# QK^T in 64-row matmuls from wave 40 on, and a TensorE order that plans for changes of row count

One core of one Trainium2 chip; the metric is the device time of one execution in microseconds (us), the median of the runs of one kernel. "Before" is an already tuned attention kernel, "after" the same kernel with the change.

## The reference

```python
B, H, S, D = 1, 32, 2048, 640          # Dh = D // H = 20
def reference(q, k, v, t):             # q, k, v: (1, 32, 2048, 20) bf16; t: (32,)
    eps = 1e-6
    qn = q / (jnp.sqrt((q * q).sum(axis=-1, keepdims=True)) + eps)
    kn = k / (jnp.sqrt((k * k).sum(axis=-1, keepdims=True)) + eps)
    logits = jnp.einsum('bhqd,bhkd->bhqk', qn, kn) * t[None, :, None, None]
    attn = _softmax(logits, axis=-1)
    return jnp.einsum('bhqk,bhkd->bhqd', attn, v)
```

There are 32 heads of 2048 x 2048 logits, each from a contraction over only 20 channels (padded to 32). The exp of 134 million logits is most of the work.

## The kernel before

Logits are made in units of 128 keys x 512 queries. Two engines turn them into weights. ScalarE takes "waves" of three units (a 128x1536 exp from the PSUM tile `psA`, which has two slots). VectorE takes three or four "tiles" of four units per head through one PSUM bank, `psD`, and computes exp with integer arithmetic. TensorE makes the logits (QK) and multiplies the weights with v (PV, four 128*32 matmuls side by side into `psO`; in the trace of before all four start within 10 ns in the median). Every instruction is a task in a small list scheduler, run when the program is built. It gives each engine a static, in-order list, so an engine that falls behind its plan makes the others wait (in the trace of before VectorE waits 18.6 us for `psD`).

A unit's 32 channels lie in one of four 32-partition bands g. The moving operand `qz[g]` holds q in band g and zeros in the other bands, so a unit can be computed with 32, 64 or 128 array rows with the same result. In a wave of three units two lie in different halves of the array: this "pair" runs as two 64-row matmuls side by side (their starts are 3 ns apart in the median of that trace). The third, the "single", uses 128 rows, as do VectorE's units.

```python
    # the scheduler picks the next task of an engine by priority (lower first)
                _, _, t = heapq.heappop(ready[e])
                t.start = now
                t.end = now + t.dur
                if e == "PE":
                    kind = t.name[:2]                 # "qk" or "pv"
                    if kind != last_pe[0]:
                        t.end += 0.09                 # planned cost of a change
                    last_pe[0] = kind
    # ... cut ...
        def qk_mm(eng, h, r, g, dst, rows):
            # ... cut: choice of slot, lhsT (keys) ...
            p0 = 32 * g // rows * rows
            ps = slice(p0, p0 + rows)
            mov = qz[bt][ps, g, :] if rows > 32 else qkT[bt][ps, 0:512]
            # ... cut ...
            return eng.matmul(dst, lhsT, mov, tile_position=(p0, 0))
    # ... cut: add_wave(w), with pair = two neighbouring units in different halves ...
            qks = [add("PE", f"qkA{w}", lambda e, tk, part=part: f_qk(e, part, 32 if plain else 64 if part is pair else 128),
                       PE_MM * (1 if plain or part is pair else len(part)), deps, due_a(us[0]) - 100) for part in parts]
    # ... cut: add_dgroup, VectorE's tile j, unit g ...
                    qk = add("PE", f"qkD{j}.{g}", lambda e, tk, h=h, r=r, g=g, j=j: qk_mm(
                        e, h, r, g, psD[:, :], 128 if j else 32), PE_MM, dep, due - 50)
    # ... cut: loads of q (in four parts), k and v, all issued in order from one queue ...
                    lds[h].append(dma("SP", f"ldq{h}", dst, src, war, pri, f"q{b}", lat=2.5))
```

## Time and profile before

| | before |
|---|---|
| time, median of 3 runs (lowest to highest) | 755.69 us (755.17 to 755.82) |
| span of the profiled run, mean granted TensorE clock | 753.2 us, 1.000 |
| exp waves; shortest and median distance of their starts | 539; 1330 and 1330 ns |
| loss of ScalarE: sum of (distance - 1330 ns), before wave 40 / from wave 40 on | 3.7 / 14.3 us |
| distances over 1400 ns | 100 |

In this trace ScalarE never starts two waves closer than 1330 ns, so I take the sum of what the distances have above it as what ScalarE lost to waiting. The starts are those of the trace's timeline.

Five lines of the kernel before's timeline (start us, us, engine, line, op, rows*columns of the array used, shapes, count; in brackets the idle time before and what ended it) show what a change of shape costs.

```profile
402.12 0.10 PEld L415 LDWEIGHTS psA<-qz,qkT 64*128 64x128 bf16 x2 [0.26 <-ACT p_ring L489]
402.13 0.39 PE L415 MATMUL psA<-qz,qkT 64*128 64x512 bf16 x2
...
402.45 0.39 PE L415 MATMUL psA<-qz,kR 128*128 128x512 bf16 x1
...
402.77 0.40 PE L424 MATMUL psO<-p_ring,vaug 128*32 128x512 bf16 x4
...
402.99 0.39 PE L424 MATMUL psO<-ss,vaug 128*32 128x512 f16 x4
```

From the pair to the single, and from the single to PV, the starts are 0.32 us apart; from PV to PV they are 0.22 us apart. (The record of one matmul is 0.39 us long and those of PV start 0.22 us apart, so records overlap; I count the distances of the starts.) The waits view puts this time down to "issue", for which it sees no releaser (us in total, times, longest).

```profile
PEld psA L415 <- issue: 169.9, 711, 0.4
PEld psA L415 <- ACT p_ring L489: 124.4, 356, 1.0
...
DVE xt L522 <- PE psD L415: 18.6, 41, 1.2
```

### The profile page before, as it was taken

Reading aid. Unit: us, or ns where it says so; the run is one execution under the profiler, and the core shown is the slowest. Engines: PE = TensorE matmul, PEld = TensorE weight load, DVE = VectorE, ACT = ScalarE, POOL = GpSimd, SP = SyncE. Lnnn points to the kernel's source line nnn. Section 1 sums busy time; section 2 is a strip of 40 time slices with the busy share of each in tenths; the row PEclk is TensorE's granted clock in tenths of the full one; section 3 lists DMA queues with packets and bytes.
Section 4 is the critical chain, followed back from the end, with each engine's and each line's share of the span. In section 5 each row is a group of like instructions: output and inputs, shape, how many; then the busy total and the mean of one; then the engine's idle time right before and its main releaser. Section 6 shows DMA issues by size and latency. Waiting matters only on the chain.

```text
span 753.2 us, 12434 instructions
## 1 busy us (share of the span) xinstructions
PE 702.4 (93%) x4960; PEld 194.6 (26%) x4960; DVE 719.6 (96%) x1209; ACT 731.7 (97%) x541; POOL 9.2 (1%) x24
## 2 busy tenths in 40 slices
PE   1999999999999999999999999999999999999997
PEld 0222222222222222222222222222222222222222
DVE  7799999999999999999999999999999999999997
ACT  3899999999999999999999999999999999999997
POOL 4000000000000000000000000000000000000000
PEclk9999999999999999999999999999999999999999
DMA  5533242323423242250323413234141332413000
GB/s 76 84 38 54 42 75 33 73 22 68 53 37 72 24 81 29 55 66 19 78 24 66 55 29 71 21 66 54 37 76 9 82 39 46 70 28 72 5 5 5
DMA packets 197929, 36.49 MB, mean 48 GB/s; under 512 B 173680, under 2 KB 197872, under 8 KB 197872
## 3 DMA queue, kind: packets, MB, share of 16 engines
q1 hardware_dynamic: 197728, 35.62, 29.6%
q8 instruction: 39, 0.64, 0.4%
q14 instruction: 18, 0.15, 0.1%
q10 hardware_dynamic: 144, 0.08, 0.1%
HBM read 7.87 MB, written 2.62 MB: 14 GB/s over the span
## 4 chain that ended last, share of the span: by engine, by line
ACT 59%; PE 23%; DVE 15%; DMA 1%; issue 1%; SPq 0%; DVEq 0%
ACT p_ring L489 59%; PE psA L415 11%; PE psO L424 8%; DVE xt L522 6%; PE psD L415 5%; DVE tt L536 4%; DVE mm L534 1%; DVE ee L530 1%; DVE ss L532 1%; DVE sq L320 1%; DVE rs_sum L322 1%; DMA kR<-kx 1%; SPq L234 0%; DVE qkn L348 0%; DMA qk_sb<-in_k_dram 0%
## 5 line engine op out<-in xcount | busy, mean ns | idle before, releaser
L489 ACT ACTIVATE p_ring<-psA 128x1536 bf16<-128x1536 f32 x539 | 730.2, 1523 | 15.7 <-PE psA L415 14.5
L415 PE MATMUL psA<-qz,kR 64*128 64x512 bf16 (+1 forms) x1209 | 319.0, 389 | 13.9 <-ACT p_ring L489 10.7
L522 DVE TENSOR_SCALAR xt<-psD 128x512 int16<-128x512 f32 x432 | 295.4, 684 | 23.1 <-PE psD L415 18.6
L424 PE MATMUL psO<-p_ring,vaug 128*32 128x512 bf16 x1616 | 152.1, 388 | 0.6 <-DVE oT L436 0.4
L415 PEld LDWEIGHTS psA<-qz,kR 64*128 64x128 bf16 (+1 forms) x1209 | 83.4, 94 | 225.3 <-issue 128.4
L415 PE MATMUL psA<-qz,qkT 64*128 64x512 bf16 (+1 forms) x392 | 128.6, 388 | 4.0 <-ACT p_ring L489 3.2
L536 DVE TENSOR_TENSOR tt<-xt,mm 128x2048 f16<-128x2048 f16 x108 | 131.0, 1213 | 0.2
L415 PE MATMUL psD<-qz,kR 128*128 128x512 bf16 x321 | 124.0, 386 | 6.0 <-DVE xt L522 3.8
L530 DVE TENSOR_SCALAR ee<-xt 128x2048 int16<-128x2048 int16 x108 | 73.7, 682 | 0.4
L534 DVE TENSOR_SCALAR mm<-xt 128x2048 int16<-128x2048 int16 x108 | 73.8, 684 | 0.0
L532 DVE TENSOR_SCALAR ss<-xt 128x2048 int16<-128x2048 int16 x108 | 73.7, 683 | 0.0
L424 PEld LDWEIGHTS psO<-p_ring,vaug 128*32 128x32 bf16 x1616 | 38.5, 94 | 84.6 <-issue 74.9
L415 PEld LDWEIGHTS psA<-qz,qkT 64*128 64x128 bf16 (+1 forms) x392 | 31.3, 94 | 68.9 <-issue 41.5
L415 PEld LDWEIGHTS psD<-qz,kR 128*128 128x128 bf16 x321 | 31.0, 97 | 65.8 <-DVE xt L522 43.6
L424 PE MATMUL psO<-tt,vaug 128*32 128x512 f16 x432 | 42.8, 386 | 3.4 <-DVE tt L536 2.0
L424 PE MATMUL psO<-ee,vaug 128*32 128x512 f16 x432 | 43.1, 389 | 1.5 <-DVE ee L530 1.3
L415 PE MATMUL psD<-qz,qkT 128*128 128x512 bf16 x107 | 41.5, 388 | 2.2 <-DVE xt L522 1.1
L424 PE MATMUL psO<-ss,vaug 128*32 128x512 f16 x432 | 42.7, 386 | 0.1
L320 DVE TENSOR_TENSOR sq<-qk_sb 128x640 f32<-128x640 bf16 x32 | 26.0, 813 | 0.9 <-DMA qk_sb<-in_q_dram 0.9
L322 DVE TENSOR_REDUCE rs_sum<-sq 128x32 f32<-128x640 f32 x32 | 25.7, 804 | 0.1
L348 DVE TENSOR_TENSOR qkn<-qk_sb,rs_r 128x640 bf16<-128x640 bf16 x31 | 25.2, 815 | 0.1
L436 DVE STREAM_TRANSPOSE oT<-psO 128x512 f32<-128x512 f32 x32 | 22.7, 709 | 2.1 <-PE psO L424 2.1
(36 smaller groups left out, 117.9 us busy)
## 6 DMA issues: line engine op xcount, KB each, us to landing
kR<-qkT SPq DMA_DIRECT2D x62, 96.0 KB, 2.1
qz<-qkT SPq DMA_DIRECT2D x128, 32.0 KB, 1.9
kR<-qkT SPq DMA_DIRECT2D x62, 64.0 KB, 2.0
qk_sb<-in_k_dram SPq DMA_DIRECT2D x32, 80.0 KB, 2.1
vaug<-in_v_dram SPq DMA_DIRECT2D x32, 80.0 KB, 3.3
qk_sb<-in_q_dram SPq DMA_DIRECT2D x124, 20.0 KB, 2.5
out_dram<-o_stage SPq DMA_DIRECT2D x31, 80.0 KB, 1.9
kR<-qkT SPq DMA_DIRECT2D x62, 32.0 KB, 1.9
```

What stands on the lines that cost most here:

```text
L320: s1 = dv("sq", lambda e, tk, x=x: e.tensor_tensor(sq[:, :, :], x[:, :, :], x[:, :, :], ALU.mult), 0.86, lds[h] + last_sum)
L322: sums.append(dv("sum", lambda e, tk, i=i: e.tensor_reduce(rs["sum"][:, 2 * R * i:2 * R * (i + 1)], sq[:, :, :], AXIS_X, ALU.add), 0.86, [ ...
L348: norm[h] = dv("norm", lambda e, tk, x=x, b=b, i=i: e.tensor_tensor(qkn[b][:, :, 0:D], x[:, :, :], bc(rs["r"][:, 2 * R * i:2 * R * (i + 1) ...
L415: return eng.matmul(dst, lhsT, mov, tile_position=(p0, 0))
L424: last = eng.matmul(psO[32 * g:32 * g + 32, :], vaug[h % NV][:, r_of(g), :], rhs_of(g), start=start, stop=False, skip_group_check=True, ti ...
L436: trO[h] = add("DVE", f"tr{h}", lambda e, tk: e.transpose(oT[:, :, :].rearrange("p r d -> p (r d)"), psO[:, :]), 0.63, [lambda: pv_users[h ...
L489: act[w] = add("ACT", f"exp{w}", lambda e, tk: e.activation(p_ring[:, p0 * 512:p0 * 512 + n], psA[:, slot * WAVE * 512:slot * WAVE * 512 + ...
L522: t1_prev[0] = add("DVE", f"t1.{j}.{g}", lambda e, tk, o=o: e.tensor_scalar(xt[sx][:, o:o + 512], psD[:, :], X_MUL, X_ADD, ALU.mult, ALU.a ...
L530: te = dv("e", lambda e, tk: e.tensor_scalar(ee[se][:, 0:w], x, 0x7C00, KE_BITS, ALU.bitwise_and, ALU.bitwise_or), 0.533, t1s + old("e", NE))
L532: t5 = dv("s", lambda e, tk: e.tensor_scalar(ss[se][:, 0:w], x, float(SHIFT - 4096), None, ALU.add), 0.533, t1s + old("s", NE))
L534: tm = dv("m", lambda e, tk: e.tensor_scalar(mm[sm][:, 0:w], x, 0x3FF, 0x3800, ALU.bitwise_and, ALU.bitwise_or), 0.533, t1s + old("m", NM))
L536: tT = dv("T", lambda e, tk: e.tensor_tensor(tt[se][:, 0:w], x.bitcast(FP16), mm[sm][:, 0:w].bitcast(FP16), ALU.mult), 1.067, [tm] + old(" ...
```

## The change

Intent: from wave 40 on all QK of ScalarE's waves, and from tile 8 on all QK of VectorE, is done with 64 rows, so that TensorE doesn't change its row count between pair and single. The scheduler learns that 64-row QK ("q2"), 128-row QK ("qk") and PV ("pv") are three kinds, and it prefers a task of the kind that ran last if its priority is no more than 0.3 heads later. VectorE's QK loses its very high priority.

```diff
+    SWITCH = 0.3
 # ... cut ...
-                _, _, t = heapq.heappop(ready[e])
+                if e == "PE":
+                    x = min(ready[e], key=lambda r: (r[0] + (0.0 if r[2].name[:2] == last_pe[0] else self.SWITCH), r[1]))
+                    ready[e].remove(x)
+                    heapq.heapify(ready[e])
+                    t = x[2]
+                else:
+                    _, _, t = heapq.heappop(ready[e])
 # ... cut ...
+    LIGHT = 40
+    LD = 8
 # ... cut ...
+            light = w >= LIGHT
-            qks = [add("PE", f"qkA{w}", lambda e, tk, part=part: f_qk(e, part, 32 if plain else 64 if part is pair else 128),
+            qks = [add("PE", f"q{'2' if part is pair or light else 'k'}A{w}", lambda e, tk, part=part: f_qk(e, part, 32 if plain else 64 if part is pair or light else 128),
 # ... cut ...
-                    qk = add("PE", f"qkD{j}.{g}", lambda e, tk, h=h, r=r, g=g, j=j: qk_mm(
-                        e, h, r, g, psD[:, :], 128 if j else 32), PE_MM, dep, due - 50)
+                    qk = add("PE", f"q{'k' if j < LD else '2'}D{j}.{g}", lambda e, tk, h=h, r=r, g=g, j=j: qk_mm(
+                        e, h, r, g, psD[:, :], (128 if j < LD else 64) if j else 32), PE_MM, dep, due - 0.5)
```

More of the change, by code (lines that the diff above doesn't have):

```diff
@@ L44 @@
     SEM_LAT = {"PE": 0.18, "ACT": 0.15, "DVE": 0.10, "POOL": 0.15, "SP": 0.0}
+    SWITCH = 0.3
     def __init__(self):
         self.tasks = []
+        self.nsw = 0
     def add(self, eng, name, fn, dur, deps=(), pri=0.0, lat=0.0, dma=None):
@@ L100, in schedule @@
                         t.end += 0.09
+                        self.nsw += 1
                     last_pe[0] = kind
```

## The prediction

The 96 ns are the difference of two distances in the trace of before, 322 - 226 ns. 45 + 24 = near 69 us of TensorE time, and 9.7 us, about two thirds of the 14.3 us of late waves, taken off 755.7 us gives 746.0 us.

> **What bounds the kernel now.** Three engines are almost full: ScalarE 97%, VectorE 96%, TensorE 93% (busy shares of the page). ScalarE sets the floor. In the timeline its 539 exp waves start no closer than 1330 ns, and more than half of the intervals are exactly that. 538 x 1.330 = 715.5 us, and the measured distance from the first to the last start is 733.5 us, so only 18.0 us is lost. Of that, 3.7 us falls before wave 40, where the change starts, and 14.3 us after it. What lies before the first wave (14.1 us) and after the last (4.2 us) stays. So at most about 14 us (1.9%) can be won. VectorE has similar room: in the stretch from 30 to 747 us it is busy 694 of 717 us, and its largest wait is for TensorE's psD (18.6 us, 41 times, by the waits).
>
> **What the losses come from.** TensorE runs late. Starts of successive matmuls in the timeline are 226 ns apart when the row/column shape stays (128*32 after 128*32, or 128*128 after 128*128), and about 322 ns when it changes: 64-row pair to 128-row single 322 (501 times), PV to 64-row pair 322 to 332, single to PV 308 to 320. [...] About 1670 changes of this kind cost some 160 us of TensorE. The plan knows of 0.09 us at a change between QK and PV, but of none between 64 and 128 rows, so the real TensorE falls behind its static order, and ScalarE and VectorE wait.
>
> **What the change does.** From wave 40 on (93% of the waves) QK has one shape. The change inside a wave goes (465 x 96 ns = 45 us) and that from a 128-row single to the next pair (about 250 x 96 ns = 24 us): near 69 us of TensorE time. A wave's QK becomes available 96 ns sooner. A lone 64-row matmul should take as long as a 128-row one. Planning with a switch penalty should also save some QK/PV changes. VectorE's QK loses its near-absolute priority over PV (due-50 becomes due-0.5), which may delay a few psD.
>
> **On the critical path.** Per wave TensorE needed about 1234 of 1330 ns; it will need about 1100 (estimates from slot counts times 226 ns plus changes times 96 ns). Nearly all of the 69 us is therefore off the critical path; what counts is how many of the 14 us of late waves go. I expect about two thirds: in-order queues and the single psD buffer keep some waits, and VectorE must then be 98% full.
>
> **Prediction.** 746.0 us (-1.3%), 80% range 741.5 to 752.5. Faster by over 2%: 0.06; within 2%: 0.91; slower by over 2%: 0.03.
>
> **What would show it.** TensorE busy falls from 93% towards 85 to 88%; single-after-pair spacing 322 becomes 226 ns; intervals of exp over 1400 ns fall from 100 to a third or half; VectorE's wait for psD falls under 10 us; exp still 1330 ns; DMA unchanged; ScalarE's share reaches 98%.
>
> **What would make it wrong.** If 64-row matmuls on the same half can't hide their weight load (spacing stays near 320 ns), nothing is won. If the new order delays psD or PV so that VectorE starves, it is flat or slower.

## More of the kernel before

From the page of the kernel before: span, busy time of each engine with its share and its instructions, the granted clock in 40 slices (9 is 90% or more), the chain that ended last, and two groups (busy us, mean ns of one, then idle time before them and what ended it).

```profile
span 753.2 us, 12434 instructions
...
PE 702.4 (93%) x4960; PEld 194.6 (26%) x4960; DVE 719.6 (96%) x1209; ACT 731.7 (97%) x541; POOL 9.2 (1%) x24
...
PEclk9999999999999999999999999999999999999999
...
ACT 59%; PE 23%; DVE 15%; DMA 1%; issue 1%; SPq 0%; DVEq 0%
...
L489 ACT ACTIVATE p_ring<-psA 128x1536 bf16<-128x1536 f32 x539 | 730.2, 1523 | 15.7 <-PE psA L415 14.5
L415 PE MATMUL psA<-qz,kR 64*128 64x512 bf16 (+1 forms) x1209 | 319.0, 389 | 13.9 <-ACT p_ring L489 10.7
```

Three engines are nearly full at once, and TensorE holds 23% of the chain: waves are often released by it and not by ScalarE itself.

## The result, and the profile after

| | before | after |
|---|---|---|
| time, median (lowest to highest) | 755.43 us (754.94 to 755.82, 4 runs) | 757.07 us (755.01 to 766.85, 4 runs) |
| ratio of the fast runs | 1 | 1.0013, 95% interval 0.9992 to 1.0034 |
| mean granted clock | 1.000 (profiled run) | 0.979, 0.979, 0.973 (fast); 0.955 (the run of 766.85 us, slow) |
| loss of ScalarE, before wave 40 / from wave 40 on | 3.7 / 14.3 us | 2.9 / 14.7 us |
| distances over 1400 ns | 100 | 40 |

A ratio is the mean time of one kernel's fast runs over that of the other's of the same rounds, so it is not quite the ratio of the medians quoted. The slow run is left out of what follows.

So nothing was won: 0.1% slower, within noise. Yet the mechanism is there. First the same lines of the page, of the kernel after.

```profile
span 753.0 us, 12422 instructions
...
PE 646.4 (86%) x4954; PEld 160.9 (21%) x4960; DVE 718.0 (95%) x1209; ACT 727.3 (97%) x541; POOL 9.2 (1%) x24
...
PEclk9999999999999899999989999988999999999999
...
ACT 85%; PE 5%; DVE 4%; SPq 2%; DMA 2%; issue 1%; ACTq 0%; DVEq 0%
...
L502 ACT ACTIVATE p_ring<-psA 128x1536 bf16<-128x1536 f32 x539 | 725.7, 1776 | 20.2 <-PE psA L427 18.5
L427 PE MATMUL psA<-qz,kR 64*128 64x512 bf16 (+1 forms) x1208 | 290.0, 392 | 51.5 <-ACT p_ring L502 44.1
```

TensorE is 56 us less busy, and now waits for ScalarE. Its part of the chain fell from 23% to 5%. But the row of the clock has eights in it that were not there before. Two lines of the timeline of the kernel after show pair and single.

```profile
239.54 0.39 PE L427 MATMUL psA<-qz,kR 64*128 64x512 bf16 x2
...
239.76 0.38 PE L427 MATMUL psA<-qz,qkT 64*128 64x512 bf16 x1
```

They are now 0.22 us apart, although the single uses rows that the pair has just used. The waits view of the kernel after:

```profile
PEld psA L427 <- ACT p_ring L502: 215.1, 469, 1.2
...
PEld psA L427 <- issue: 19.2, 57, 0.8
...
DVE xt L535 <- PE psD L427: 15.4, 37, 0.9
...
DVE sq L332 <- DMA qk_sb<-in_q_dram: 4.4, 3, 2.2
```

The unexplained "issue" time fell from 169.9 us to 19.2 us: so most of these waits stood at the changes of row count that are gone. The fall is more than what was saved. A wait of 0.23 us at a change also holds what the weight loader idles without one (some 0.13 us, an estimate: 226 ns between starts less 94 ns of loading), and a part is now put down to ScalarE (215.1 us, 124.4 before). The last line is new in size (0.9 us in 3 waits before): twice VectorE waits about 2 us for a late load of q.

Where did the gain go? The windows view of the kernel after, in stretches of 3.4 us around 384 us, gives busy us (and instructions) of PE, PEld, DVE, ACT and POOL, then the granted clock, DMA share and GB/s.

```profile
380.50:383.90 3.40, 2.99 (x23) 0.76 (x23) 3.30 (x6) 3.40 (x4) 0.00 (x0) 1.00 0.78 82
383.90:387.30 3.40, 1.29 (x9) 0.27 (x8) 1.16 (x3) 3.40 (x3) 0.00 (x0) 1.00 0.67 42
387.30:390.70 3.40, 3.02 (x16) 0.49 (x16) 3.07 (x6) 1.86 (x3) 0.00 (x0) 0.50 0.00 0
390.70:394.10 3.40, 2.06 (x18) 0.54 (x15) 3.40 (x5) 3.40 (x3) 0.00 (x0) 0.99 0.00 0
394.10:397.60 3.50, 3.50 (x22) 0.71 (x21) 3.29 (x9) 2.90 (x3) 0.00 (x0) 0.51 0.02 5
```

In the stretch from 383.9 us VectorE waits 2.24 us for q, its QK, in order in TensorE's list, is held up behind it (2.89 us before the weight load of `psD` at 387.68 us, by the timeline), and TensorE is busy for only 1.29 of 3.40 us. In the next stretch the granted clock is 0.50, and ScalarE is busy for 1.86 of 3.40 us. After one more lean stretch (390.7 us: 2.06 us busy) the clock falls again. A waiting load isn't needed for this, as the same view around 90 us shows.

```profile
86.90:90.30 3.40, 2.68 (x23) 0.72 (x20) 3.23 (x5) 3.40 (x4) 0.00 (x0) 1.00 0.54 109
90.30:93.70 3.40, 1.95 (x17) 0.43 (x11) 3.40 (x6) 3.40 (x4) 0.00 (x0) 1.00 0.27 68
93.70:97.20 3.50, 3.50 (x23) 0.61 (x20) 3.50 (x7) 3.50 (x3) 0.00 (x0) 0.51 0.33 82
```

Here VectorE and ScalarE are busy all through the second stretch; TensorE had less to do (1.95 us busy), and it lost its clock for the next 3.4 us.

The trace's clock record has 30.7 us at half clock in six stretches (3.4, 3.4, 6.8, 3.4, 3.4 and 10.2 us), not counting the start and the end of the program. The record of before has none. Only 1.0 and 0.5 occur in the two records. In that of after every stretch between the first fall and the one at the end of the program, at half or at full clock, is a multiple of 3.413 us (half clock 3.413, 6.827 and 10.240 us; full clock from 3.413 to 238.933 us).

I split ScalarE's loss from wave 40 on into distances near such a stretch (from 0.5 us before it to 5 us after it) and all others:

| | near a stretch at half clock | elsewhere | sum |
|---|---|---|---|
| before | 0 | 14.3 us in 498 distances | 14.3 |
| after | 10.8 us in 44 distances | 3.9 us in 454 distances | 14.7 |

Elsewhere the loss fell by 10.4 us, a little more than predicted; 10.8 us were given back near the half-clock stretches. That is an account, not yet a cause, and the 10.8 us also hold what VectorE's two waits for q cost by themselves (see cells_only below). The rival is that the new order itself (with its late q loads and demoted psD) makes the waits, and that the clock only follows.

### The profile page after: what moved, and what is told of

The parts are those of the page before. It is cut to its first block, busy times and chain, and to the rows that moved or that the text cites. A ratio compares the mean times of both kernels' runs of the same rounds, so it can differ in the third digit from the quotient of the medians.

```text
span 753.0 us, 12422 instructions
## 1 busy us (share of the span) xinstructions
PE 646.4 (86%) x4954; PEld 160.9 (21%) x4960; DVE 718.0 (95%) x1209; ACT 727.3 (97%) x541; POOL 9.2 (1%) x24
## 2 busy tenths in 40 slices
DMA packets 197929, 36.49 MB, mean 48 GB/s; under 512 B 173680, under 2 KB 197872, under 8 KB 197872
## 4 chain that ended last, share of the span: by engine, by line
ACT 85%; PE 5%; DVE 4%; SPq 2%; DMA 2%; issue 1%; ACTq 0%; DVEq 0%
ACT p_ring L502 85%; PE psA L427 2%; SPq L246 2%; PE psO L436 2%; DVE xt L535 1%; PE psD L427 1%; DMA qk_sb<-in_q_dram 1%; DVE tt L549 1%; DMA kR<-kx 0%; DVE sq L332 0%; DVE rs_sum L334 0%; DMA qk_sb<-in_k_dram 0%; DVE mm L547 0%; DVE kx L399 0%; DVE ss L545 0%
## 5 line engine op out<-in xcount | busy, mean ns | idle before, releaser
L427 PE MATMUL psA<-qz,kR 64*128 64x512 bf16 (+1 forms) x1208 | 290.0, 392 | 51.5 <-ACT p_ring L502 44.1
L535 DVE TENSOR_SCALAR xt<-psD 128x512 int16<-128x512 f32 x432 | 295.6, 684 | 20.6 <-PE psD L427 15.4
L436 PE MATMUL psO<-p_ring,vaug 128*32 128x512 bf16 x1616 | 155.0, 394 | 2.3 <-DVE oT L448 1.0
L427 PE MATMUL psA<-qz,qkT 64*128 64x512 bf16 (+1 forms) x392 | 130.4, 390 | 16.0 <-ACT p_ring L502 14.1
L427 PE MATMUL psD<-qz,kR 64*128 64x512 bf16 (+1 forms) x318 | 123.8, 389 | 9.3 <-DVE xt L535 7.7
L427 PEld LDWEIGHTS psA<-qz,kR 64*128 64x128 bf16 (+1 forms) x1209 | 59.7, 94 | 184.4 <-ACT p_ring L502 165.3
L427 PEld LDWEIGHTS psD<-qz,kR 64*128 64x128 bf16 (+1 forms) x321 | 30.0, 93 | 86.1 <-DVE xt L535 63.5
L427 PE MATMUL psD<-qz,qkT 64*128 64x512 bf16 (+1 forms) x105 | 41.5, 395 | 1.9 <-DVE xt L535 1.1
```

The lines of the kernel that those rows point to most:

```text
L436: last = eng.matmul(psO[32 * g:32 * g + 32, :], vaug[h % NV][:, r_of(g), :], rhs_of(g), start=start, stop=False, skip_group_check=True, ti ...
L535: t1_prev[0] = add("DVE", f"t1.{j}.{g}", lambda e, tk, o=o: e.tensor_scalar(xt[sx][:, o:o + 512], psD[:, :], X_MUL, X_ADD, ALU.mult, ALU.a ...
```

## The experiments

Theory 1: the faster TensorE idles more, its clock is halved, and that eats the gain. Theory 2: the new order and its waits eat it. All kernels but before come from the edits shown; all results were correct. "Clock" is the mean granted clock of the single runs; "near/elsewhere" is the loss split as above, in the profiled run. The kernel before always stayed at 0.998 to 1.000. Two of the five calls ran on chips where the first exp starts late in every kernel I profiled there (17.4 us and more in place of 14.1 to 15.2 us) and before mostly takes 757.7 to 759.7 us, so times are compared within a call.

| run | ratio to before (95%) | median us | clock | near / elsewhere us |
|---|---|---|---|---|
| rows_only | 0.9988 (0.9930 to 1.0046) | 755.87 | 0.976 to 0.995 | 10.0 / 4.9 |
| plan_only | 0.9989 (0.9974 to 1.0004) | 754.39 | 0.996 to 0.998 | 0 / 12.2 |
| fill64 | 0.9974 (0.9956 to 0.9993) | 753.14 | 0.987 to 0.993 | 7.4 / 6.7 |
| due50 | 0.9987 (0.9972 to 1.0002) | 754.26 | 0.978 | 9.4 / 4.2 |
| quad_same | 1.0015 (0.9987 to 1.0044) | 758.76 | 0.990 to 0.992 | 7.9 / 6.5 |
| loads | 1.0157 (1.0120 to 1.0194) | 770.31 | 0.936 to 0.949 | 24.5 / 2.4 |
| quad_loads | 0.9904 (0.9870 to 0.9939) | 751.07 | 0.999 to 1.000 | 0 / 6.5 |
| a_only | 1.0080 (1.0037 to 1.0123) | 764.38 | 0.986 to 0.995 | 5.6 / 10.2 |
| after_again | 1.0052 (1.0028 to 1.0077) | 759.23 | 0.960 to 0.979 | 12.2 / 4.8 |
| quad_loads_again | 0.9884 (0.9870 to 0.9899) | 746.96 | 0.998 to 1.000 | 0 / 6.7 |
| cells_only | 0.9993 (0.9978 to 1.0008) | 754.36 | 0.988 to 0.995 | 2.5 / 9.9 |
| cells_loads | 0.9890 (0.9877 to 0.9903) | 747.52 | 0.998 to 1.000 | 0 / 6.5 |
| quarter_loads | 0.9880 (0.9865 to 0.9896) | 746.50 | 0.998 to 1.000 | 0 / 6.5 |
| cells_loads_again | 0.9888 (0.9874 to 0.9902) | 747.47 | 0.998 to 0.999 | 0 / 6.5 |
| plan_loads | 1.0024 (1.0010 to 1.0037) | 757.50 | 0.995 to 0.997 | 0 / 12.1 |
| before_loads | 1.0014 (1.0001 to 1.0027) | 756.86 | 0.999 to 1.000 | 0 / 15.3 |
| rowq_loads (fast runs) | 0.9955 (0.9938 to 0.9972) | 755.28 | 0.979 to 0.990 | 8.6 / 5.6 |
| quarter_loads_again | 0.9900 (0.9887 to 0.9913) | 750.76 | 0.998 to 1.000 | 0 / 6.5 |

### Rows or order?

**rows_only**: the kernel before with its own order; only the row counts change.

```diff
-  f_qk(e, part, 32 if plain else 64 if part is pair else 128)
+  f_qk(e, part, 32 if plain else 64 if part is pair or w >= 40 else 128)
-  e, h, r, g, psD[:, :], 128 if j else 32)
+  e, h, r, g, psD[:, :], (128 if j < 8 else 64) if j else 32)
```

> The kernel before with its own order of instructions on every engine; only the QK of waves from 40 on and of VectorE's tiles from 8 on is in 64-row matmuls. Theory 1 (the clock ate the gain: TensorE is faster, idles more, and in its leanest windows the granted clock halves for 3.4 us and more): spacing of single after pair falls to 226 ns, the mean granted clock falls to 0.96 to 0.99, time within 1% of before. Theory 2 (the new order ate the gain, by the late q loads and the demoted psD): the clock stays above 0.99 and the time is 744 to 749 us.

The order of before shows the same falls, as the row of the clock on its page shows, and its profiled run has no wait of VectorE for q over 0.5 us from 40 us on.

```profile
PEclk9999969999999999999999999999999999899999
```

Its four runs line up with the clock they were granted: 748.88 us at 0.995, 755.04 at 0.983, 756.71 at 0.977 and 757.76 at 0.976. One program with one order thus differs by 8.9 us, in step with the clock. So the gain is lost without the new order, and theory 2 falls as the main cause. That the low clock makes the waits, and not the waits the low clock, four runs side by side don't show; the runs loads and quad_loads below do.

**plan_only**: the kernel after with `LIGHT` and `LD` set so high that no further QK uses 64 rows.

> The changed kernel's planning (change of row count known, psD priority lowered) with the row counts of before. Theory 1: TensorE is as busy as before, so the clock stays 1.00; the time moves little, 750 to 757 us. Theory 2: the order is at fault, so this is slower than before, over 758 us, with VectorE waits for the q loads as in the changed kernel.

The clock record of the profiled run shows no fall but that at the end of the program (which is why the mean is 0.996 to 0.998), and the time hardly moves: the new order neither harms nor helps measurably. Elsewhere it loses 12.2 us, not far from the 14.3 us of before, which fits a TensorE that is still late.

**due50**: the kernel after, with VectorE's QK at `due - 50` again.

> The changed kernel with VectorE's QK back at its high priority (due-50). Theory 1: the clock still falls (0.96 to 0.99), time 752 to 760 us. Theory 2: with psD first again the time falls under 750 us.

The falls stay (0.978 in every run), and the time is that of before. The demoted psD isn't the cause. Nor need it be the late loads: this run has no wait of VectorE for q over 0.5 us from 40 us on, and still lost 9.4 us near its half-clock stretches.

**a_only**: `LD` so high that VectorE's tiles keep 128 rows; ScalarE's waves have 64.

> Of the change only ScalarE's waves are in 64 rows, VectorE's tiles stay in 128 rows (planned as such). More cells at work than in the changed kernel (planned share under 38% in 0.2% of the windows), more changes of row count: one to three falls of the clock, 0.99 to 0.998, time 748 to 754 us.

Slower by 0.8%, which I hadn't expected. There was one stretch of 13.7 us at half clock, around a wait of 2.0 us before VectorE's squaring of q and k, and the span ends 10.6 us after the last exp has started (5.6 us in before): this plan leaves VectorE with more to do at the end. As its plan differs, it says little of the clock.

### Fillers

If the clock falls for want of work, give TensorE work. **fill64** adds matmuls with zero weights into `psO`, which change no result, where the plan has a gap in TensorE's list and the planned load around it is low. They stand between two PV of the same head, so no other engine reads `psO` at that time.

```diff
+  z_f = [memset("POOL", zw[:, :], 0.0, 0.1, -97), memset("POOL", xf[:, :], 0.7, 0.3, -97)]
   # after a task of TensorE, as often as plan_fill decided (0.8 of a planned gap, where under 70% of
   # the 3.4 us around it are planned busy):
+  for _ in range(self.fill.get(t.seq, 0)):
+      self.filler(eng)
+  prog.filler = lambda e: e.matmul(psO[:, :], zw[0:64, :], xf[0:64, :], start=False, stop=False,
+                                   skip_group_check=True, tile_position=(0, 0))
```

> The changed kernel with about 190 filler matmuls (zero weights, 64 rows, adding zero to psO) put where the plan has TensorE idle and the planned load around it is low. Theory 1: fewer or no stretches at half clock (mean granted clock over 0.99) and the time falls to 745 to 750 us, although TensorE does more work. Theory 2: order and waits are those of the changed kernel, so 755 us or slower. If the clock still falls as often, a filler of this kind is not what the clock is granted for.

More work made it slightly faster, but not 745 to 750 us. The half-clock stretches left all follow waits of VectorE for a q load (1.9 us at 202, 2.3 us at 387 and 1.4 us at 523 us): a static filler can't fill a gap that the plan doesn't know of.

Then I laid windows of 3413 ns, from its clock record, over the trace of the kernel after, and compared those that were followed by half clock with those that were not. A matmul counts for 215 ns from its start (an estimate: the least distance of two successive PV in the traces of before and after). From 45 to 740 us there are 194 windows at full clock, six of them followed by half clock. The share of time in which the array was in use doesn't separate them: it is 24 to 50% in the six, and three of the others had 46 to 48%. The share of the array's cells at work does: 18 to 37% in the six, 38% or more in all others. **quad_same** tests that: the same places, but the filler is four 128*32 matmuls side by side, for which the plan counts the same 216 ns (in the trace of after, 64-row QK starts 216 ns after a 64-row single in the median; PV starts 215 ns or more after PV).

```diff
-  e.matmul(psO[:, :], zw[0:64, :], xf[0:64, :], start=False, ..., tile_position=(0, 0))
+  [e.matmul(psO[32 * g:32 * g + 32, :], zw[:, 0:32], xf[:, :], start=False, ..., tile_position=(0, 32 * g)) for g in range(NG)]
```

> The fillers of the run fill64, same number and same places, but as a quad of 128*32 matmuls (zero weights, all 128 rows and 128 columns of the array at work) in place of one 64*128 matmul: the same 216 ns of time, twice the cells. If the clock follows the time that TensorE is busy, it stays at 0.987 to 0.993 as with fill64. If it follows the share of the array at work [...], the planned windows never fall under 40% and only windows around unplanned waits for q loads can: 0.993 to 1.000, time 746 to 752 us.

Inconclusive, and a miss of mine: the clock was 0.990 to 0.992, as with fill64. Again the falls came at waits before VectorE's squaring of q and k (1.7 us at 205 and 2.0 us at 392 us), where the kind of filler can't matter.

### The late loads

**loads** takes those waits away by planning: q and k are loaded before v, their latency is planned with 4.0 us and preparation starts earlier.

```diff
-  ... f"q{b}", lat=2.5)
+  ... f"q{b}", lat=4.0)
-  war, pri + 0.1, f"v{bv}"
+  war, pri + 1.1, f"v{bv}"
-  LEAD = 2.4
+  LEAD = 2.6
```

> The changed kernel without fillers; q and k loads are planned earlier and before the v loads, so that VectorE no longer waits 2 us for a q load. If those waits are what costs the gain, 745 to 750 us. If the share of the array at work is, the clock falls as often or more (the planned share is under 38% in 7% of the windows, 3% in the changed kernel): clock 0.95 to 0.98, time 753 to 762 us.

The plainest answer to theory 2: most of the waits for q are gone, elsewhere the loss is the lowest of all (2.4 us in 396 distances), and yet the kernel is 1.6% slower than before, because it runs 95.6 us of the profiled run at half clock. (Why the earlier loads leave more lean windows isn't shown; the plan had them, as the expectation says.) From its page:

```profile
PEclk9999989799979999999979989998997977979999
```

**quad_loads** has both: the fillers of quad_same with their places taken from the new plan, and the earlier loads.

> Both: fillers as quads and earlier loads. Theory 1 expects the full clock (0.997 to 1.000) and 745 to 749 us, over 0.8% faster than before. Theory 2 (order and waits) expects no more than quad_same or loads alone.

Full clock, and 1.0% faster. Here the effects don't add: fillers alone give 0, loads alone +1.6%, both -1.0%. The program of loads and that of quad_loads differ in the fillers alone, which change no result and release no other engine; this added work took the time from 770.31 to 751.07 us, and the clock from at most 0.949 to at least 0.999. That shows the direction: the low clock costs the time.

### A version that beats both

The next call ran on a chip where before took 755.48 us. **after_again** is the changed kernel unaltered, **quad_loads_again** repeats quad_loads. **cells_only** and **cells_loads** (without and with the earlier loads) place quads so that every 3.4 us of the plan has at least 46% of the array at work: 127 and 136 fillers in place of some 190.

> The changed kernel, unaltered, again, on the chip of the next three: 5 to 9 stretches at half clock, mean clock 0.955 to 0.98, within 0.5% of before in the runs that count as fast; the time of single runs goes down with the granted clock, about 3 us for each 0.01 of it.

> The same kernel as quad_loads: clock 0.998 to 1.000, 0.7 to 1.1% faster than before. With the head of the span as in the first profiles (first exp at 14 us) 746 to 749 us.

> The changed kernel with quads placed by the planned share of the array at work (target 46% in every 3.4 us; 127 fillers in place of 190), loads as in the changed kernel. The clock falls only around the unplanned waits for q loads: one to three falls, 0.985 to 0.997, 749 to 755 us.

> The same placing (136 fillers) with the earlier loads. If the share of the array at work is the whole cause, the clock is 0.995 to 1.000 and the time is as quad_loads or up to 3 us better, because fewer fillers stand in the way: 744 to 749 us.

The changed kernel was 0.5% slower this time, at 0.960 to 0.979; two of its runs at 0.960 and 0.961 took 762.8 and 761.6 us. Time and clock go together less neatly than in rows_only (one run took 757.4 us at 0.972, another 761.1 us at 0.973), so the 3 us for each 0.01 that I expected is not a rule. cells_only came in as expected (one fall, 754.36 us), and it shows what the half-clock split hides. Its clock is nearly kept, yet it gains nothing. In its timeline VectorE waits for q at 240.4 us:

```profile
242.48 0.83 DVE L377 TENSOR_TENSOR sq<-qk_sb 128x640 f32<-128x640 bf16 x1 [2.10 <-DMA qk_sb<-in_q_dram]
```

The windows view of the stretch after it:

```profile
243.60:247.00 3.40, 3.04 (x28) 0.84 (x28) 3.40 (x7) 2.78 (x3) 0.00 (x0) 1.00 0.48 47
```

The clock is full (1.00), and ScalarE still loses 1.5 us in the waves from 244 to 253 us (by the distances of their starts). The waits at 200 and 384 us cost 1.2 us and, before the clock fell at 389.5 us, 1.9 us. So the late loads are a second cause of their own: by these figures the two in the changed kernel account for some 3.4 of its 10.8 us (an estimate, 1.5 + 1.9), which leaves some 7.4 us for the low clock.

cells_loads, without those waits, runs at full clock at 747.5 us, 1.1% under before. Its page:

```profile
span 744.6 us, 13505 instructions
...
PE 670.6 (90%) x5498; PEld 169.5 (23%) x5504; DVE 717.0 (96%) x1209; ACT 725.7 (97%) x541; POOL 9.8 (1%) x26
...
PEclk9999999999999999999999999999999999999999
```

TensorE issues 5498 - 4954 = 544 matmuls more than the kernel after (136 quads), and is busier by 24 us, yet the program is 8.4 us shorter (span).

Does the gain belong to the 64 rows, or only to the earlier loads? **plan_loads** and **before_loads** have the earlier loads with the row counts of before, under the new and the old planning.

> plan_only with the earlier loads: new planning, row counts of before. If the earlier loads alone bring the gain, 746 to 749 us at full clock. If the 64-row matmuls are needed, TensorE stays some 93% busy and late: 752 to 757 us at full clock.

> The kernel before with the earlier loads only. If the earlier loads alone bring the gain, 746 to 749 us. Otherwise 753 to 758 us, as the kernel before had almost no wait for q loads (0.9 us in all); full clock in either case.

Neither gains; both are 0.1 to 0.2% slower, without a fall of the clock before the end. For plan_loads a part of that is its end: it stops 10.4 us after its last exp has started, before after 5.6 us. Even with those 4.7 us taken off it would be at 752.8 us (an estimate), and its loss elsewhere, 12.1 us, is nearly twice that of cells_loads. The earlier loads alone are not the gain; the 64 rows are needed, and so is the clock.

### Columns, rows or time

**quarter_loads** is cells_loads with one 128*32 matmul per filler: the same planned time, a quarter of the cells. **cells_loads_again** is its partner on the same chip.

```diff
-  [e.matmul(psO[32 * g:32 * g + 32, :], zw[:, 0:32], xf[:, :], ..., tile_position=(0, 32 * g)) for g in range(NG)]
+  e.matmul(psO[0:32, :], zw[:, 0:32], xf[:, :], ..., tile_position=(0, 0))
```

> cells_loads with the fillers in the same 136 places, but one 128*32 matmul each in place of four side by side: the same row count, the same 216 ns, a quarter of the cells. If the clock follows the time TensorE is in use, it stays at 0.998 to 1.000 and the time at 746 to 749 us as in cells_loads. If it follows the cells at work (planned share under 37.5% in 1.4% of the windows), there are several falls: clock 0.96 to 0.99, 750 to 760 us.

> The same kernel as cells_loads, as partner on the same chip: clock 0.998 to 1.000, 1.0 to 1.2% faster than before.

My theory of cells fell here. By cells several falls were due (1.4% of the planned windows were under 37.5%), and the clock stayed at 0.998 to 1.000 in all four runs: with three quarters of the fillers' columns gone, the clock was still that of cells_loads (0.998 to 1.000). That left two readings: mere time in use, against which the trace of after spoke (24 to 50% in the six windows, 46 to 48% in three that kept the clock), or rows. **rowq_loads** turns the filler around: 32 rows by 128 columns, the same number of cells and the same planned time. **quarter_loads_again** is the partner.

```diff
-  e.matmul(psO[0:32, :], zw[:, 0:32], xf[:, :], ..., tile_position=(0, 0))
+  e.matmul(psO[:, :], zw[0:32, :], xf[0:32, :], ..., tile_position=(0, 0))
```

> cells_loads with one 32*128 matmul for each of its 136 fillers: the same number of cells as in quarter_loads and the same time, but 32 rows in place of 128. If the clock follows the rows at work over time (a lone 64-row matmul counting half, columns not counting), several falls: clock 0.96 to 0.99, 750 to 760 us. If it follows mere use of time, full clock and 746 to 749 us as quarter_loads. Some of a difference of under 2 us can come from the added changes of tile shape.

> The same kernel as quarter_loads: clock 0.998 to 1.000, 1.0 to 1.3% faster than before.

With 32-row fillers the clock falls again (0.979, 0.986 and 0.990 in the fast runs; the other three runs count as slow and are left out); with 128-row fillers of the same size it doesn't, in four of four runs (0.998 to 1.000). Before took 758.21 us on this chip, so 750.76 us is again 1.0% faster. Two windows from each, laid on the grid of the clock record; first rowq_loads:

```profile
202.30:205.70 3.40, 2.93 (x17) 0.67 (x15) 3.40 (x6) 3.40 (x4) 0.00 (x0) 1.00 0.85 49
205.70:209.10 3.40, 3.40 (x15) 0.46 (x15) 2.16 (x5) 3.03 (x3) 0.00 (x0) 0.50 0.00 0
```

and quarter_loads, a lean window at 471 us:

```profile
471.30:474.70 3.40, 2.56 (x14) 0.73 (x14) 2.87 (x5) 3.40 (x4) 0.00 (x0) 1.00 0.18 12
474.70:478.10 3.40, 3.31 (x22) 0.82 (x21) 3.40 (x9) 3.40 (x4) 0.00 (x0) 1.00 0.00 0
```

With 2.93 of 3.40 us busy the first lost its clock in the next window (0.50); with 2.56 of 3.40 us busy the second kept it (1.00). In these two busy time was no guide to the clock.

For the trace of after, three measures of a window, each matmul counted for 215 ns from its start as above:

| measure of a window at full clock | the six followed by half clock | the 188 others |
|---|---|---|
| share of time with any matmul | 24.2 to 49.9% | 45.5% and more |
| share of cells (rows x columns) | 17.6 to 36.7% | 37.7% and more |
| share of rows (a lone 64-row matmul counts half, a pair whole, PV whole) | 17.8 to 37.0% | 38.1% and more |

Counted from 60 ns after each start, the figures move by up to 1.7 points and the picture stays. Cells and rows both separate the windows of this one trace, so it is the two experiments with turned fillers that tell them apart: at the same cells and the same planned time, 32*128 fillers went with 0.979 to 0.990 in the fast runs and 128*32 fillers with 0.998 to 1.000. By the same measure of rows, before has 66.7% on average and 46.6% in its leanest window (203 windows, none followed by half clock); after has 53.5% on average. By time they have 67.0 and 65.5% on average: TensorE is in use for nearly as much of the time as before, with fewer rows, so "idles more" in theory 1 was not the point.

## Why the prediction was wrong

- **ScalarE's floor and the room of 14 us**: right. The floor stayed at 1330 ns, and no version lost less than 8.9 us in all.
- **Changes of shape cost 96 ns**: right. 322 ns became 226 ns in the median, "issue" before QK weight loads fell from 169.9 to 19.2 us, TensorE fell from 93% to 86%, within 85 to 88%.
- **A 64-row matmul on the rows just used hides its weight load**: right (226 ns from pair to single, with weight loads of 94 ns in the mean), so the failure I had named first did not occur.
- **Distances over 1400 ns fall to a third or half of 100**: right, 40.
- **VectorE's wait for psD under 10 us, and ScalarE at 98%**: wrong, 15.4 us and 97%. The clock isn't the reason: cells_loads, at full clock, still has 14.1 us and 97%. What keeps this wait long stays open.
- **DMA unchanged**: right for the bytes (36.49 MB in both), wrong for the timing: two loads of q came about 2 us too late for VectorE in this plan.
- **"Nearly all of the 69 us is therefore off the critical path; what counts is how many of the 14 us of late waves go. I expect about two thirds"**: this is the step that failed. Away from half-clock stretches 10.4 of 14.3 us (73%) did go. But the step treats TensorE time off the critical path as free and the granted clock as given; the prediction doesn't mention the clock. The change saved time without taking work away, and it halved the rows of every single: the share of rows at work fell from 67% to 54% on average (an estimate, with the 215 ns above), and to 18 to 37% in the six windows before the falls. The clock was then halved for 30.7 us of the profiled run, and 10.8 us came back as waits there, some 3.4 us of them (an estimate, from cells_only) by the late loads of q and the rest, as far as is known, by the clock.
- **746.0 us** is nearly what the change gives at full clock: 746.5 to 747.5 us in three kernels that keep it (quad_loads_again, cells_loads and quarter_loads, where before took 755.48 us). That supports the sizes, but these kernels also have earlier loads and fillers, so it isn't the same program. The nearest without either is the run of rows_only at a clock of 0.995, 748.88 us.

What stays open: no experiment looked for a limit; the ranges in the table are those of one trace with six falls, and some matmul records can be missing from it. Why the clock falls, and whether it goes with rows or with something that goes with them, can't be told from here. Why the same program has more half-clock stretches in one run than in another isn't settled either; where its windows happen to lie is a guess.

## What to carry to other kernels

Before making an engine leaner whose granted clock has been seen to fall, look at its leanest stretches (here of 3.4 us) and not at its average, and see how many rows each matmul there uses: rows of zeros may not be mere waste (here 32*128 fillers went with a clock of 0.979 to 0.990, 128*32 fillers with 0.998 to 1.000). After such a change read the granted clock first; here a figure as near to 1 as 0.979 went with the loss of most of the gain. Then look for waits of another kind: the late loads took the rest. If the lean stretches are known when the program is built, a few matmuls with zero weights in full-row shape, placed in planned gaps, went with a kept clock here (0.998 to 1.000) and no cost in time (cells_loads, 747.52 us), but they helped only once the unplanned waits were gone too (cells_only, without the earlier loads: 754.36 us).
